# Another order of the first half of a hand-written instruction list, in attention and MLP on one core

## The chip, the core and the metric

The kernel runs on one core of one Trainium2 chip. The metric is device time in microseconds of one execution. A core has five engines with an instruction stream each: TensorE (PE in the profile, which also shows its weight loads as PEld), VectorE (DVE), ScalarE (ACT), GpSimd (POOL) and SyncE (SP, which here only issues DMAs). Each engine takes its instructions in order; engines wait for each other by semaphores.

## What is computed

Batch 8, 8 heads, 576 positions, head size 64; the model width is 512 and the MLP's 2048. The inputs are float32.

```python
scores = scale * np.matmul(q, k.transpose(0, 1, 3, 2))
cum = np.cumsum(np.maximum(s, 0.0), axis=-1)
bias = -(cum[:, :, :, None] - cum[:, :, None, :])
scores = np.where(causal, -1e9, scores + np.minimum(bias, 0.0))
attn = softmax(scores); x = np.matmul(attn, v)      # heads side by side: [8, 576, 512]
xn = (x - mu) / np.sqrt(var + 1e-06) * g_ln
out = x + np.maximum(xn @ w_ch1, 0.0) @ w_ch2
```

## The kernel before

All of it is in `fast_path` (lines 28 to about 1365). Work is cut into small steps, each a Python function that emits a few instructions. A dictionary `STEPS` (L1186) gives each step a short name, and a string `PLAN` (L1274, 1238 words) lists the steps in the order in which they are emitted. The order is written out: inside `tc.manual_schedule()` every engine executes its instructions in the order of emission, and nothing rearranges them. A word such as `E.k.4.1:D` is a step's name, its arguments, and after the colon the engine (A is ACT, D is DVE, P is POOL):

```python
for word in PLAN.split():
    step, _, eng = word.partition(":")
    name, *args = step.split(".")
    args = [int(c) if c.isdigit() else c for c in args]
    STEPS[name](*args, *([E[eng]] if eng else []))
```

The batches are treated in three ways.

- Batch 0, by tiles of 128 positions, while the data comes in. The sums of the gate (`relur`, `relu`, `scan` L292) are split into three bfloat16 pieces (`hi`, `mid`: L308, or L306 where ACT does it; `sub`, `lo`: L311), of which one scan has three parts (columns 0 to 128, to 256, to 576). `tc` transposes them on PE (L275), `bc` puts them beside q and k in `rowb` (DVE, L281 and L285), `ck` and `cq` cast the first tile of k and q (ACT, L140). `T` transposes a tile of q and k on PE (L944), `e` evicts it from PSUM (L140 on ACT, L142 on DVE), `S` makes scores (L966, mask L974), `x` the exponentials (ACT, L983), `V` the weighted sums (L1024), `N` divides them (DVE, L1049), `B` and `L` are the layernorm's statistics and its result xn (L710), `X` transposes xn on PE (L743), `y` evicts it, `M` is a piece of the first MLP layer (L1068), `r` its relu. `Sk`/`xk` are the scores and exponentials of the last 64 keys. `m` and `me` are memsets, the latter on POOL (L1235).
- Batch 1, by heads. `Q` transposes k or q of a head pair on PE (L322), `E` evicts it. `s` makes a head's scores in three PSUM banks (L390), their exponentials on ACT (L401) and a causal mask on POOL (L410); `d` the last 64 keys of a pair of heads (L426, L437, mask L440). `v` is the weighted sum (L583), `n` the division (DVE, L595, L597, L604). `aug` and `a3` copy bias rows by DMA. `O2`, `F` and `G` are cast, transposes (L360) and eviction for pairs of batch 2.
- Batches 2 to 7, by pairs of heads. The gate becomes a weight on v: `wr`, `wT`, `wx` make the weights, `vm` multiplies v by them on POOL (L232), `vo` writes the weights beside it (L244, L245). `lr` and `lv` load k, q, v in float32 (SP), `cr` casts k and q on POOL (L217), `tr` transposes them by DMA, `tk` copies the last keys on POOL (L144). `B2` is a burst of six banks of scores of a pair (L548), `bx` one bank's exponentials (ACT, L553), `bm` one mask (POOL, L492); `sd`, `se`, `sm` are the same for the last 64 keys. `Y` is the weighted sum (L627), `K` its division. `ga`, `la`, `l` are layernorm statistics and xn (L669, L710), `R` the reciprocal deviation of batch 0 (DVE L683, then POOL L684), `Da` and `D` its transposition by DMA on SP.

The MLP of the batches before is a queue of units. A word `u` or `U` takes the next unit: either "h", four matmuls of the first layer (L761) with their relu eviction, or "y", four matmuls of the second layer (L780); the last "y" of a tile adds the residual into `yo` (DVE, L792) and writes it out by a DMA on SP. The two words differ only in the engine of the relu eviction: ACT for `u` (L752), DVE for `U` (L750).

```python
"U": lambda: run_units(1, "dve"),
"u": lambda: run_units(1, "act"),
```

Most waits come from buffers. Until the word `to`, PSUM has two banks "m" (T, M, units), three "s" (scores), two "t" (Q, X, V, F, transposes) and one "o" (v); from `to` on there are two "m" (second layer) and six "s" (scores, first layer). A step that takes a bank waits until the step that used it before has been evicted. `lp` and `w2` issue DMAs on POOL's own stream (L183, L255), in which the masks stand too.

Of the kernel before, what the change touches and what calls it, by code (L numbers as in the profile page):

```python
# [30 lines left out]
def fast_path(  # L31
# [1147 lines left out]
    def raise_flag(count, ones, n):  # L1179
# [120 lines left out]
        la.1.4 B2.10 bx.10.0 K.9.0 bx.10.3 bx.10.4 bx.10.2 bx.10.5 cr.3.4.0 bm.10.3 bx.10.1 Y.9.1 U  # L1300
        K.9.1 u u tr.3.2.4 U u tr.3.4.5 bm.10.1 Y.10.1 lv.3.1 bm.10.0 B2.11 bx.11.0 bx.11.4 lv.3.2
        bx.11.5 lv.3.3 K.10.1 bm.10.2 Y.10.0 K.10.0 bm.11.2 ga.2.0.0 lv.3.4 bx.11.2 bm.11.0 La.4 bx.11.1
        u ga.2.1.2 ga.2.0.3 U u tk.3 cr.4.1.1 lr.4.2 bx.11.3 Y.11.0 K.11.0 bm.11.3 u sd.3 U bm.11.1 u
        se.3 ga.2.0.1 lr.4.3 cr.4.0.1 vm.3.1:P Y.11.1 K.11.1 lv.4.0 lv.4.1 vm.3.4:P lr.4.4 u ga.2.1.0 u
        B2.12 bx.12.0 vm.3.2:P U bx.12.4 bm.12.2 ga.2.1.1 bx.12.1 lv.4.2 ga.2.2.0 cr.4.2.1 ga.2.2.1
        ga.2.1.3 lv.4.3 la.2.0 la.2.1 cr.4.0.0 bx.12.5 bm.12.3 vm.3.3:P cr.4.1.0 ga.2.2.2 bx.12.3
        bm.12.1 u bx.12.2 bm.12.0 u u u B2.13 bx.13.5 bx.13.1 ga.2.0.2 la.2.2 u bx.13.0 cr.4.4.0 sm.3
        bx.13.4 tr.4.0.2 ga.2.2.3 u u bx.13.3 u Y.12.0 la.2.3 Da.2.0 bx.13.2 bm.13.0 K.12.0 u u B2.14
        cr.4.4.1 tr.4.4.5 bx.14.2 Y.12.1 K.12.1 lv.4.4 bx.14.1 bm.13.2 bx.14.3 vo.4:P bx.14.4 u u u
# [279 lines left out]
```

## Time and profile before

| | us |
|---|---|
| Three runs | 346.55, 347.80, 348.76 (median 347.80) |
| Profiled execution, own time | 347.71 |
| Its span, first to last instruction | 346.2 |
| PE waits by semaphore, the longest single one | 1.5 (before any data is there) |
| PE's waits after 8 us that the trace lists, together | about 4 |

Busy time of the engines over 40 equal slices of 8.65 us; a digit is tenths, 9 is 90% or more:

```profile
PE   5999999989999999999999999999999999999994
DVE  6598798847585587356653764567358614533512
ACT  4587889768655676357646773486434204202200
POOL 8898577696577774865685277350301001000000
```

The list's first 639 words fill the time to about 135 us, that is the first 15 to 16 slices. "Idle before" in a row of a timeline is the time in square brackets in which the engine did nothing, and behind the arrow stands what ended it; starts are counted from the first instruction.

### The profile page before, as it was taken

The page shows a single profiled execution, that of the slowest core. Times are in us where ns is not written, and L with a number is a line of the kernel's source. Part 1 is how long each engine was busy: PE and PEld are TensorE (multiplying, and loading weights), DVE is VectorE, ACT ScalarE, POOL GpSimd, SP SyncE. Part 2 cuts the span into 40 slices and gives each one's busy share as a digit, 9 for nine tenths or more (in the row PEclk, how much of TensorE's full clock was granted, in tenths as well). Part 3 has the DMA queues.
Part 4 walks back from the last instruction along what each step waited for, and adds up shares of the span by engine and source line. Part 5 has one row for each costly group of instructions (what it writes and reads, how often), then busy time and mean ns, then how long its engine had stood idle before and what let it go on. Part 6 is the DMA issues. An engine that isn't in the chain of part 4 may idle for free.

```text
span 346.2 us, 8012 instructions
## 1 busy us (share of the span) xinstructions
PE 332.7 (96%) x3066; PEld 186.3 (54%) x3092; DVE 206.2 (60%) x592; ACT 185.5 (54%) x343; POOL 167.8 (48%) x306
## 2 busy tenths in 40 slices
PE   5999999989999999999999999999999999999994
PEld 2898866545545555555555555555545444444443
DVE  6598798847585587356653764567358614533512
ACT  4587889768655676357646773486434204202200
POOL 8898577696577774865685277350301001000000
PEclk9699999999999999999999999999999999999999
DMA  9999999899999999998775956500410041011022
GB/s 148 181 192 176 203 206 204 171 247 218 199 203 232 221 222 180 224 230 187 154 197 145 236 104 159 138 2 2 118 66 0 20 134 45 2 66 56 0 64 66
DMA packets 147485, 48.61 MB, mean 140 GB/s; under 512 B 135184, under 2 KB 142896, under 8 KB 147440
## 3 DMA queue, kind: packets, MB, share of 16 engines
q1 hardware_dynamic: 121616, 38.34, 51.3%
q0 software_dynamic: 24304, 8.92, 21.8%
q10 hardware_dynamic: 1520, 0.79, 0.9%
q8 instruction: 25, 0.41, 0.5%
q14 instruction: 20, 0.16, 0.2%
HBM read 37.11 MB, written 9.44 MB: 134 GB/s over the span
## 4 chain that ended last, share of the span: by engine, by line
PE 89%; POOL 4%; DMA 4%; issue 1%; DVE 0%; ACT 0%; POOLq 0%
PE py L780 36%; PE ph L761 34%; PE pot L627 7%; DMA v_bf<-in_v_dram 2%; PE sa L548 2%; PE ph L1068 2%; DMA w_bf<-in_moe_w_ch_dram 2%; PE sc L548 2%; PE sb L548 2%; PE pot L583 1%; POOL rowb L179 1%; POOL kq L906 1%; PE trp L360 1%; PE trqk L322 1%; PE sb L390 1%
## 5 line engine op out<-in xcount | busy, mean ns | idle before, releaser
L780 PE MATMUL py<-w_bf,hT 128*128 128x512 bf16 (+2 forms) x583 | 128.3, 368 | 2.3 <-DVE yo L792 0.8
L761 PE MATMUL ph<-xT,w_bf 128*128 128x512 bf16 x480 | 109.8, 380 | 0.0
L752 ACT ACTIVATE hT<-ph 128x512 bf16<-128x512 f32 x97 | 58.1, 603 | 80.8 <-PE ph L761 79.4
L780 PEld LDWEIGHTS <-hT 128*128 128x128 bf16 x608 | 56.1, 98 | 61.7 <-issue 1.3
L761 PEld LDWEIGHTS <-w_bf 128*128 128x128 bf16 x544 | 50.9, 98 | 56.4
L492 POOL TENSOR_SCALAR_AFFINE_SELECT er<-er 128x256 bf16<-128x256 bf16 x96 | 38.6, 416 | 60.9 <-ACT er L553 45.9
L792 DVE SCALAR_TENSOR_TENSOR yo<-py,rstd,xb 128x512 f32<-128x512 f32 x32 | 24.0, 751 | 50.0 <-PE py L780 42.2
L750 DVE TENSOR_SCALAR hT<-ph 128x512 bf16<-128x512 f32 x39 | 26.8, 690 | 26.8 <-PE ph L761 25.9
L553 ACT ACTIVATE er<-sb 128x512 bf16<-128x512 f32 x48 | 28.2, 609 | 21.1 <-PE sb L548 15.2
L553 ACT ACTIVATE er<-sa 128x512 bf16<-128x512 f32 x48 | 28.6, 609 | 13.7 <-PE sa L548 10.9
L232 POOL TENSOR_TENSOR v_bf<-rowtmp,wt 128x512 bf16<-128x512 f32 (+1 forms) x30 | 32.4, 1086 | 2.3 <-DMA rowtmp<-in_v_dram 2.2
L553 ACT ACTIVATE er<-sc 128x512 bf16<-128x512 f32 x48 | 28.7, 613 | 4.1 <-PE sc L548 4.1
L627 PEld LDWEIGHTS <-er 128*128 128x128 bf16 x672 | 25.7, 97 | 9.5 <-issue 0.4
L627 PE MATMUL pot<-v_bf,er 128*128 128x66 bf16 x672 | 28.0, 194 | 0.1
L684 POOL TENSOR_TENSOR rstd<-rstd,mhalf 128x4 f32<-128x4 f32 (+1 forms) x8 | 8.8, 1098 | 38.2 <-DVE rstd L683 34.4
L644 DVE TENSOR_REDUCE sums<-pot 128x5 f32<-128x10 f32 x48 | 7.9, 166 | 30.5 <-PE pot L627 30.2
L710 DVE SCALAR_TENSOR_TENSOR xn<-xb,mv,gb 128x512 bf16<-128x512 f32 x28 | 24.3, 870 | 1.0
L217 POOL CAST kq<-rowtmp 128x512 bf16<-128x512 f32 (+1 forms) x30 | 19.8, 669 | 9.6 <-DMA rowtmp<-in_k_dram 8.5
L669 DVE BATCH_NORM_STATS2 stats<-xb 128x6 f32<-128x128 f32 (+1 forms) x84 | 23.7, 322 | 0.4
L647 DVE TENSOR_TENSOR xb<-pot,rinvs 128x256 f32<-128x256 f32 x48 | 20.4, 425 | 1.6
L548 PEld LDWEIGHTS <-kq 64*128 64x128 bf16 x360 | 11.3, 95 | 10.0 <-issue 4.7
L983 ACT ACTIVATE er<-st 128x512 bf16<-128x512 f32 x24 | 13.1, 604 | 4.4 <-PE st L974 3.0
(169 smaller groups left out, 397.0 us busy)
## 6 DMA issues: line engine op xcount, KB each, us to landing
out_dram<-yo SPq DMA_DIRECT2D x32, 256.0 KB
rowtmp<-in_v_dram SPq DMA_DIRECT2D x24, 256.0 KB
rowtmp<-in_k_dram SPq DMA_DIRECT2D x20, 256.0 KB
rowtmp<-in_q_dram SPq DMA_DIRECT2D x20, 256.0 KB
w_bf<-in_moe_w_ch_dram POOLq DMA_DIRECT2D x8, 512.0 KB, 9.0
kp<-in_k_dram POOLq DMA_DIRECT2D x8, 144.0 KB, 8.5
qp<-in_q_dram POOLq DMA_DIRECT2D x8, 144.0 KB, 8.9
v_bf<-in_v_dram POOLq DMA_DIRECT2D x8, 128.0 KB, 7.3
```

The costliest lines, as they stand in the source:

```text
L232: e.tensor_tensor(out=v_bf[b % 2][0:pn, t, :, 0:D], in0=loaded.pop(("v", b, t))[0:pn], in1=wt[0:pn, t, b, :].unsqueeze(2).to_broadcast([pn ...
L492: nc.gpsimd.affine_select(out=out, in_=out, compare_op=ALU.is_ge, fill=0.0, base=0, pattern=pattern, channel_multiplier=-1,)
L548: nc.tensor.matmul(a, lhsT=lhsT, rhs=rhs, start=True, stop=True)
L553: nc.scalar.activation(out=er[:, 2 * n % 4 + i, o : o + 512], in_=bank["B", n].pop((name, i)), func=ACT.Exp, scale=scale,)
L627: nc.tensor.matmul(pot[:, t, :], lhsT=cols, rhs=v_bf[b % 2][:, kb, h, :], start=(kb == 0), stop=(kb == t),)
L669: nc.vector.bn_stats(out=st[b][:, t, part, :], in_=x_tiles(b)[t][:, lo:hi])
L710: nc.vector.scalar_tensor_tensor(out=xn, in0=tiles[t], scalar=mvs[b][:, t, 0:1] if b > 0 else mean0[:, t : t + 1], in1=gb, op0=ALU.subtrac ...
L750: nc.vector.tensor_scalar_max(out=dst, in0=ph, scalar1=0.0)
L752: nc.scalar.activation(out=dst, in_=ph, func=ACT.Relu)
L761: nc.tensor.matmul(ph, lhsT=w1_bf[:, kd, fb * P : (fb + 1) * P], rhs=xT[:, :, kd, :], start=(kd == 0), stop=(kd == KD - 1),)
L780: nc.tensor.matmul(py[t], lhsT=hT[:, fb, t * P : (t + 1) * P], rhs=w2_bf[:, fb, c0:c1], start=(fb == 0), stop=(fb == FB - 1),)
L792: nc.vector.scalar_tensor_tensor(out=yo, in0=py[t], scalar=rs, in1=x[:, c0:c1], op0=ALU.mult, op1=ALU.add)
```

## The change

Only `PLAN` is edited. Of its 1238 words the last 599, from `qm` on, are the same. The 639 words before them are the same words in another order, except that seven `u` more have become `U`. Unit by unit the eviction moves from ACT to DVE in eleven places and from DVE to ACT in four (batches 0 to 2); no matmul, no load and no eviction is added or left out. Orders that are needed for buffers and data are kept. Cut to the parts that the prediction speaks of, with the rest of the lines left out:

```diff
-        relur.1 lr.3.0 relu.0 scan.0 scan.1 cq hi.0 qu.1 hi.1 sub.0 mid.0 lo.0 relur.2 sub.1 scan.2 W.2
-        tc.0 bc.0 ck.0 T.0.1 T.0.0 mid.1 lo.1 tc.1 e.0.1:D bc.1 T.1.1 hi.2 sub.2 e.0.0:A S.0.0.0 T.1.0
...
-        x.3.0.1 V.1.0 e.3.1:D qu.3 La.2 N.1.0 V.1.1 N.1.1 L.1 S.2.0.0 x.2.0.0 S.2.0.1 x.2.0.1 S.3.0.2
-        x.3.0.2 X.0 y.0:A S.3.1.2 S.2.1.1 x.2.1.1 V.2.0 N.2.0 x.3.1.2 X.1 y.1:D S.3.0.0 x.3.0.0 V.2.1
...
-        T.4.0 e.4.0:D X.2 y.2:D x.3.1.3 Q.k.4 E.k.4.0:D T.4.1 e.4.1:D x.3.1.0 S.4.0.1 x.4.0.1 S.4.0.0
-        M.0.2.0 M.0.2.2 x.4.0.0 M.0.2.3 V.3.1 E.k.4.1:D N.3.1 B.2.1 S.4.1.1 x.4.1.1 u d.8 L.3 M.0.2.1
-        Q.q.5 r.0.2:D B.1.0 s.8 u X.3 S.4.1.0 x.4.1.0 y.3:D Sk xk E.q.5.1:D E.q.5.0:A B.0.0 B.3.0 a3 u
-        v.8 qu.4 qu.5 Q.k.5 lp.9 E.k.5.0:D u E.k.5.1:D V.4.0 N.4.0 s.9 cr.3.0.1 n.8 V.4.1 N.4.1 Q.q.6
-        E.q.6.0:A u B.2.0 d.10 s.10 wr Q.k.6 E.k.6.0:D A.0 v.9 lp.10 w2.2 lr.3.1 E.k.6.1:D n.9 u U
...
-        F.k.8 v.14 ga.1.0.1 F.k.9 G.k.9:A n.14 U u A.3 R vm.2.0:P lr.3.2 v.15 cr.3.2.0 O2.k.11:A lv.2.1
...
-        F.k.11 G.k.11:A tk.2 qu.6 qu.7 F.q.10 G.q.10:A cr.3.3.1 vm.2.4:P to u lv.3.0 B2.8 bx.8.3 bx.8.0
-        vo.3:P bx.8.2 l.1 l.2 l.3 D u ga.1.0.4 u lr.4.0 lr.4.1 sd.2 se.2 sm.2 ga.1.1.4 bx.8.4 bm.8.2
+        relu.0 scan.0 lr.3.0 W.2 hi.0 sub.0 relur.1 ck.0 mid.0 lo.0 scan.1 hi.1 tc.0 sub.1 relur.2
+        scan.2 cq bc.0 mid.1 hi.2 sub.2 T.0.1 e.0.1:D mid.2 T.0.0 e.0.0:A lo.1 tc.1 lo.2 aug bc.1 T.1.1
...
+        S.1.0.0 qu.2 qu.3 T.2.1 e.2.1:D T.2.0 e.2.0:D V.0.0 V.0.1 N.0.1 x.1.1.1 m S.1.0.1 bc.4 x.1.0.0
+        S.2.1.2 x.2.1.2 x.1.0.1 N.0.0 S.2.1.1 x.2.1.1 T.3.0 e.3.0:D S.2.1.0 T.3.1 e.3.1:D V.1.0 x.2.1.0
+        W.1 V.1.1 S.2.0.0 x.2.0.0 S.2.0.2 x.2.0.2 N.1.1 S.3.0.2 x.3.0.2 S.2.0.1 x.2.0.1 B.0.1 L.0 N.1.0
+        L.1 S.3.1.2 S.3.0.1 x.3.0.1 La.6 B.1.1 X.0 y.0:A V.2.0 N.2.0 X.1 y.1:D x.3.1.2 S.3.0.0 M.0.0.0
...
+        B.3.0 X.2 qu.6 T.4.0 e.4.0:D y.2:D T.4.1 S.3.1.0 x.3.1.0 x.3.1.3 S.4.0.1 e.4.1:D M.0.2.0 M.0.2.3
+        M.0.2.1 Q.k.4 E.k.4.0:D M.0.2.2 S.4.1.1 x.4.1.1 V.3.1 N.3.1 E.k.4.1:D x.4.0.1 u S.4.0.0 x.4.0.0
+        B.2.1 Q.q.5 L.3 E.q.5.1:D r.0.2:D s.8 u d.8 E.q.5.0:A Sk xk u X.3 y.3:D S.4.1.0 x.4.1.0 v.8 n.8
+        Q.k.5 E.k.5.0:D V.4.0 N.4.0 lp.9 w2.2 w2.3 s.9 E.k.5.1:D u V.4.1 d.10 B.0.0 N.4.1 wr s.10 Q.q.6
...
+        La.3 La.2 n.11 cr.3.0.0 ga.1.0.1 A.0 lp.10 A.3 d.12 s.13 u d.14 wT s.14 A.1 v.12 n.12 U U
+        O2.k.9:A wx s.15 v.13 n.13 A.2 ga.1.0.3 U F.k.8 F.k.9 O2.q.9:A v.14 n.14 G.k.8:A ga.1.1.0 qu.7 R
+        ga.1.1.2 me vm.2.0:P O2.q.8:A lr.3.1 U u ga.1.1.3 cr.3.1.1 lv.2.1 vm.2.1:P G.k.9:A v.15 n.15
+        ga.1.2.1 F.q.9 ga.1.2.2 lr.3.2 O2.k.11:A u lv.2.2 lv.2.3 u F.q.8 cr.3.0.1 cr.3.2.1 G.q.9:A
+        cr.3.1.0 O2.q.11:A vo.2:P O2.k.10:A vm.2.3:P lv.2.4 vm.2.4:P lr.3.3 lr.3.4 G.q.8:A ga.1.0.0
+        ga.1.2.0 l.0 ga.1.2.3 vm.2.2:P cr.3.2.0 ga.1.0.2 ga.1.1.1 u u O2.q.10:A F.q.10 G.q.10:A F.k.10
+        l.1 u u u G.k.10:A F.q.11 F.k.11 G.q.11:A l.2 l.3 D tr.3.0.2 G.k.11:A tk.2 cr.3.3.1 cr.3.3.0 to
+        u lv.3.0 lv.3.1 B2.8 bx.8.0 bx.8.5 bx.8.3 bx.8.1 u bx.8.4 u u sd.2 bm.8.2 bm.8.3 bx.8.2 bm.8.0 u
+        u bm.8.1 lv.3.2 se.2 sm.2 cr.3.4.1 B2.9 bx.9.1 Y.8.1 bx.9.3 bm.9.1 bx.9.4 bm.9.2 bx.9.5 bx.9.2
...
```

More of the change, by code (lines that the diff above doesn't have):

```diff
@@ L1300, in fast_path @@
[L1300 to L1309, printed above, removed]
@@ new lines, in fast_path @@
+        bx.14.5 bx.14.1 bm.14.3 cr.4.3.1 bm.13.1 cr.4.3.0 bx.14.0 bm.14.0 bx.14.3 bm.14.1 cr.4.2.0
+        tr.4.2.4 B2.15 bx.15.0 bx.15.2 vm.4.4:P bm.15.0 bx.15.4 Y.13.1 bx.15.1 bx.15.3 bm.15.1 tk.4
+        bx.15.5 vm.4.1:P bm.15.2 U U u U U Y.14.1 K.14.1 u u bm.14.2 Y.14.0 K.14.0 K.13.1 ga.3.1.1
+        ga.3.1.0 bm.15.3 u sd.4 se.4 ga.3.0.2 u cr.5.0.0 vm.4.2:P Y.15.1 K.15.1 ga.3.0.1 vo.4:P lr.5.1
+        cr.5.1.0 B2.16 bx.16.0 bx.16.1 ga.3.1.3 bx.16.4 bm.16.2 La.4 Y.15.0 ga.3.1.2 K.15.0 bx.16.2
@@ new lines, in fast_path @@
+        lv.7.0 sm.6 ga.5.1.3 bx.24.4 bm.24.2 ga.5.2.0 u lv.7.1 La.5 ga.5.2.1 u u bx.24.2 bm.24.0
+        ga.5.1.1 U vm.6.4:P ga.5.1.0 la.5.0 bx.24.5 bx.24.1 bm.24.3 vm.7.0:P ga.5.0.4 lv.7.2 u bm.24.1
+        lv.7.3 ga.5.2.2 u u Y.24.0 Da.3.4 u u lr.7.4 cr.7.4.0 u ga.5.2.3 u cr.7.0.0 tr.7.0.2 cr.7.4.1
+        tr.7.4.5 lv.7.4 B2.25 bx.25.2 bx.25.4 vo.7:P bx.25.0 bx.25.5 bx.25.1 bx.25.3 bm.25.2 K.24.0
+        la.5.1 Y.24.1 u K.24.1 ga.5.0.2 u ga.5.1.2 la.5.2 u la.5.3 Da.5.0 cr.7.3.1 bm.25.1 u u u u
@@ L1356, in fast_path @@
+        u u u u u u u u u u u u u u u u
     """
```

110 lines of the change are left out of this document (51 added, 59 removed).

## The prediction, made before the changed kernel was run

> **What bounds the kernel now.** I read the totals first, then the waits of TensorE (PE), then the windows of its clock.
>
> ```profile
> span 346.2 us, 8012 instructions
> PE 332.7 (96%) x3066; PEld 186.3 (54%) x3092; DVE 206.2 (60%) x592; ACT 185.5 (54%) x343; POOL 167.8 (48%) x306
> PE 89%; POOL 4%; DMA 4%; issue 1%; DVE 0%; ACT 0%; POOLq 0%
> ```
>
> PE is busy for 96% of the span and holds 89% of the chain that ended last. The other four stay at 60% or less. The change leaves every matmul as it is, and the last 599 words of the list too. So it can change only what PE waits for up to about 135 us, and how long PE runs at half clock. From the trace's answer on the waits of PE, all of the span:
>
> ```profile
> PE trt L944 <- DVE rowb L285: 1.2, 1, 1.2
> PE py L780 <- DVE yo L792: 0.8, 1, 0.8
> PE trqk L322 <- DMA w_bf<-in_moe_w_ch_dram: 0.6, 1, 0.6
> PE trp L360 <- ACT kq L140: 0.5, 1, 0.5
> PE ph L1068 <- issue: 0.4, 1, 0.4
> ```
>
> (What waits, for what, us in total, times, longest.) All of these fall before 74 us, in the stretch that is reordered, and together they are 3.5 us: 1.0% of the time. A new order can hardly win more than that, apart from the clock; it can lose any amount by a new wait. The windows show the clock (busy us of the five engines, then PEclk, DMA share, GB/s):
>
> ```profile
> 4.74:8.15 3.41, 1.54 (x7) 0.48 (x5) 3.05 (x10) 2.01 (x5) 3.33 (x6) 1.00 1.66 171
> 8.15:11.57 3.42, 2.83 (x26) 2.65 (x27) 1.89 (x9) 1.65 (x3) 3.01 (x4) 0.50 2.08 184
> 11.57:14.98 3.41, 3.19 (x32) 2.87 (x32) 1.46 (x5) 1.79 (x3) 2.58 (x4) 0.50 2.38 172
> ```
>
> The clock is halved for two stretches of 3.41 us, after one in which PE was busy for 1.54 of 3.41.
>
> **The change part by part.**
>
> *The start (+0.25).* PE's first transposes, T.0.1, wait for the bias columns bc.0 on VectorE (DVE).
>
> ```profile
> 5.32 0.48 DVE L292 TENSOR_TENSOR_SCAN c_sc<-c_one,c_sc,hT 64x128 f32<-64x128 f32 x1
> 7.34 0.87 DVE L292 TENSOR_TENSOR_SCAN c_sc<-c_one,c_sc,c_in 64x320 f32<-64x320 f32 x1
> 8.14 0.16 DVE L281 COPY rowb<-trc 128x24 bf16<-128x24 bf16 x1
> 8.45 1.89 PE L944 MATMUL trt<-ident,rowb 128*68 128x128 bf16 x16 [1.25 <-DVE rowb L285]
> ```
>
> The new order puts scan.1 behind hi.0, sub.0, mid.0 and lo.0, but bc.0 still stands behind scan.2, DVE's longest piece here (0.87). The pieces ahead of bc.0 are the same; scan.1 now ends later, so hi.1 on ScalarE (ACT) and sub.1, which needs it, come later, and scan.2 with them. Followed row by row, bc.0 starts at 8.39 (an estimate). PE loses 0.25; bounds 0 and 0.5 (one more piece like scan.1, 0.48, ahead). tc.0 is done before that in both orders, and ck.0 and cq, moved on ACT, wait for their loads in both.
>
> PE then runs without a gap from 11.3 to 14.98, as now. [...]
>
> *15 to 26 us (+0.85).* The scores of batch 0 (S), their exponentials (x), sums (V, N) and the layernorm (L, X).
>
> ```profile
> 22.48 0.75 DVE L710 SCALAR_TENSOR_TENSOR xn<-xb,mean,gb 128x512 bf16<-128x512 f32 x1
> 23.29 0.40 PE L743 MATMUL trx<-ident,xn 128*128 128x128 bf16 x4 [0.27 <-DVE xn L710]
> 20.00:30.00 10.00, 9.01 (x189) 8.54 (x187) 8.39 (x28) 8.80 (x17) 9.87 (x19) 1.00 1.48 191
> ```
>
> DVE is 84% busy here, so its order tells. The memset m, bc.4, N.0.0, both e.3 and B.0.1 now stand ahead of L.0; L.1 follows L.0 and N.1.0 at once. I walked the new list word by word, each word starting when its engine is free and its inputs are done, with its duration of now: X.1 comes at about 24.5 beside 23.29 (an estimate; the times "by the walk" below are found in the same way). 0.25 of the 1.2 is the late start, 0.1 is filled by other PE work: +0.85. Bounds: 0, if the S words between fill it, and 1.6, two rows of 0.75.
>
> *26 to 58 us: waits that go (-1.85) and come (+0.75, +0.3).*
>
> ```profile
> 28.23 0.39 PE L743 MATMUL trx<-ident,xn 128*128 128x128 bf16 x4
> 29.23 0.42 PE L322 MATMUL trqk<-ident,kp 96*128 96x96 bf16 x6 [0.62 <-DMA w_bf<-in_moe_w_ch_dram]
> 35.94 0.22 PE L1068 MATMUL ph<-xT,w_bf 128*128 128x128 bf16 x1
> 36.54 1.01 PE L1068 MATMUL ph<-xT,w_bf 128*128 128x128 bf16 x15 [0.38 <-issue]
> 42.53 0.66 PE L390 MATMUL sb<-kq 68*128 68x64 bf16 x2
> 43.03 0.38 PE L390 MATMUL sc<-kq 68*128 68x320 bf16 x2
> ```
>
> Q.k.4 starts at 29.23; the four transposes before it need 0.22 of PE, so 0.78 is lost. The DMA named was long done: Q.k.4 lacks a PSUM buffer until y.2 has emptied one. In the new list T.4.0, T.4.1, S words and M.0.2.0 stand between. M's wait at 36.54 (0.54 after 35.94 plus one matmul) is for y.3, which now has the S.4.1.0 and v.8 words behind it. sc follows sb 0.50 later at two matmuls (0.22), so 0.28 goes, since a unit now parts the scores; I count 0.25 for a later head with the same pattern, an estimate. Sum -1.85; bounds -1.85 and -0.6 (Q.k.4's alone, in part). New: T.4.1 and M.0.2 behind r.0.0 and y.2, s.8 behind E.k.4.1, d.10 behind E.k.5.1, a unit's bank. Each is part of one copy (0.3 to 0.69 us), worked out as 0.1 to 0.3 each: +0.75, bounds 0 and 1.6.
>
> lp.10, two DMA issues, is moved ahead of d.12's mask on POOL; w2.2 and w2.3 ahead of those of s.9 and s.10.
>
> ```profile
> 45.23 0.64 POOL L183 DMA_DIRECT2D kp<-in_k_dram  x1
> 46.49 0.79 POOL L255 DMA_DIRECT2D w_bf<-in_moe_w_ch_dram  x1
> 51.52 0.90 POOL L410 TENSOR_SCALAR_AFFINE_SELECT er<-er 128x256 bf16<-128x256 bf16 x2 [0.74 <-ACT er L401]
> ```
>
> 2 x 0.64 = 1.28 ahead of that mask leaves it done at about 54.35 by the walk, where PE wants v.12 at 54.05: +0.3, bounds 0 and 0.9 (a mask's length). The two w2 (2 x 0.79) end at 43.6 by the walk, s.10's masks at 45.5, and PE wants v.10 at 46.9: hidden by 1.4. What SP issues (aug, a3, lr, lv) runs ahead of the list and waits only for buffers: a3, now later, has been free to go since batch 0's last scores at 35, and s.12, its user, comes after 50: hidden.
>
> *58 to 76 us (-0.85).* The casts O2, transposes F and copies G of the next batch.
>
> ```profile
> 68.40 0.38 PE L360 MATMUL trp<-ident,rowb 96*128 96x96 bf16 x5
> 69.25 0.42 PE L360 MATMUL trp<-ident,rowb 96*128 96x96 bf16 x6 [0.47 <-ACT kq L140]
> 69.72 0.81 PE L780 MATMUL py<-w_bf,hT 128*128 128x512 bf16 x3
> 73.10 1.02 PE L780 MATMUL py<-w_bf,hT 128*128 128x512 bf16 x4 [0.84 <-DVE yo L792]
> ```
>
> F.q.10 now waits for a G copy (0.63 lost between 68.40 and 69.25 beyond the five matmuls, 0.21 after it). The new list does F.q.10 earlier and parts F.k.10 from F.q.11 by four units: -0.85; bounds -0.85 and -0.2. The wait for yo at 73.10 stays: the same units come before and after `to`.
>
> *POOL behind R (+0.55).* R (pow), the weightings vm, the casts cr, me, vo.2, tk.2 and the masks bm.8, sm.2 form one queue.
>
> ```profile
> 63.72 0.61 POOL L217 CAST kq<-rowtmp 128x512 bf16<-128x512 f32 x1 [0.94 <-DMA rowtmp<-in_k_dram]
> 65.90 1.04 POOL L232 TENSOR_TENSOR v_bf<-rowtmp,wt 128x512 bf16<-128x512 f32 x1 [1.57 <-DMA rowtmp<-in_v_dram]
> 69.17 2.49 POOL L232 TENSOR_TENSOR v_bf<-rowtmp,wt 128x512 bf16<-128x512 f32 x2 [0.66 <-DMA rowtmp<-in_v_dram]
> 60.71:77.81 17.10, 15.68 (x137) 8.03 (x138) 10.92 (x24) 11.57 (x21) 13.64 (x23) 1.00 0.91 210
> L1235 POOL MEMSET c<- 128x640 bf16 x2 | 1.2, 631 | 0.0
> 78.11 0.58 PE L627 MATMUL pot<-v_bf,er 128*128 128x66 bf16 x14
> ```
>
> From R to the last of these masks POOL is busy 13.64 of 17.10; about 3.2 of the rest are three waits for DMAs. The list now also puts me (1.2) and two more casts (2 x 0.61) into this stretch: 16.0 of work. R starts at about 61.1 by the walk (behind n.14 on DVE), so the masks end at 77.1 without waits and at 80.6 with all 3.46. PE wants them for Y.8 (L627) at 77.2 by the walk, 78.11 now. The loads lr.3 and lv.2 wait for buffers that these same casts empty; vo.2, me and two casts of tiles loaded long before now stand between, which gives them time. So most waits should go: I take about a sixth, which makes +0.55. Bounds 0 and 4.4 (all waits, and another 1.0 as the pair at 69.17 shows: 2.49 where 2 x 1.04 would do).
>
> ```profile
> 69.24 1.53 DVE L710 SCALAR_TENSOR_TENSOR xn<-xb,mv,gb 128x512 bf16<-128x512 f32 x1
> ```
>
> Beside that pair L710 took 1.53 (0.75 at 22.48). [...]
>
> *Seven evictions (0).*
>
> ```profile
> L752 ACT ACTIVATE hT<-ph 128x512 bf16<-128x512 f32 x97 | 58.1, 603 | 80.8 <-PE ph L761 79.4
> L750 DVE TENSOR_SCALAR hT<-ph 128x512 bf16<-128x512 f32 x39 | 26.8, 690 | 26.8 <-PE ph L761 25.9
> ```
>
> ACT sheds 7 x 0.60 = 4.2, DVE gains 7 x 0.69 = 4.8. What hides it is that a unit takes PE longer (four matmuls at 0.22) than the copy takes, with two to six banks in turn. Uncovered, seven copies longer by 0.09 cost 0.6; where ACT is late, as much is won: bounds -0.6 and +0.6. The rest, 76 to 135 us: tr.3.4.5 moves ahead of lr.4.0 on SP, which delays batch 4's loads to about 84 by the walk, wanted at 91; Da.2.0 comes at about 107, wanted at 115. Nothing: bounds 0, since none of the waits listed lies there, and +0.84, one wait like that at 73.10.
>
> Sum: 0.25 + 0.85 - 1.85 + 0.75 + 0.3 - 0.85 + 0.55 = 0.0. The profiled execution took 347.71, 0.09 under the median of 347.8: I forecast 347.7.
>
> **The rivals.**
>
> 1. Slower: POOL's queue behind R makes Y.8 wait. It decides from masks later than 77.3. For it: 16.0 of work where 13.64 stood, and L710 beside it. Against: most of its waits were for late loads. Price 4.4 in place of 0.55: 351.6; with half, 349.3.
> 2. Faster: the old waits go (-2.7) and the new ones are covered, since many words of other PE work stand between. With start and POOL as summed: 347.7 - 0.85 - 0.75 - 0.3 = 345.8; with X.1 and POOL free too, 345.0. The clock a stretch of 3.41 earlier adds -1.7, half of it: 343.3.
> 3. The clock a stretch longer, if PE idles about 11.3: +1.7, 349.4.
> 4. The change does nothing that can be told: the forecast's own number, by another way.
>
> **How the numbers follow.** My forecast (with rival 4) has 0.50, its own range 346.2 to 349.2 from the bounds of the small terms. Rival 1 has 0.25, rival 2 0.17, rival 3 0.08. About 1% (344.2, 351.2) is what a measurement of this kernel can tell from no change. Below 344.2 lies about half of rival 2: 0.09. Above 351.2 lie the full price of rival 1, and new waits in the long list that I did not find: 0.20. The rest, 0.71, is within 1%. The range leaves out the earlier clock and the full queue with more: 344.8 to 351.6.
>
> **What would show it.** Right: T.0.1 starts at 8.6 to 8.8; X.1 near 24.5; no gaps at Q.k.4, M after Sk and F.q.10; the gap at yo stays near 0.8; masks bm.8 and sm.2 end before Y.8 starts; PEclk back at 14.98. Wrong: a gap of over 1 us ahead of Y.8 or v.12, a third halved stretch or only one, or a gap after 80 us, where I charge nothing. A gap with other work of PE in the list right behind it, which could have filled it, would also tell against the walk.

## The result and the profile after

| | before | after |
|---|---|---|
| Median of 6 runs, us | 347.88 | 351.44 |
| Lowest and highest | 346.55, 348.76 | 350.27, 352.25 |
| Profiled execution, own time and span | 347.71, 346.2 | 351.36, 349.7 |
| Its mean granted clock | 0.990 | 0.983 |

The ratio is 1.0101, with a 95% interval of 1.0070 to 1.0131: the new order is 3.6 us slower. I had forecast 347.7 and no change. (The section on the change says eleven and four for the moved evictions; it is twelve and five, net seven.)

The changed kernel's totals, and then its list of PE's waits:

```profile
span 349.7 us, 7999 instructions
PE 336.2 (96%) x3067; PEld 188.8 (54%) x3092; DVE 209.6 (60%) x599; ACT 181.2 (52%) x336; POOL 167.7 (48%) x306
```

```profile
PE trt L944 <- DVE rowb L285: 2.1, 1, 2.1
PE py L780 <- DVE yo L792: 0.8, 1, 0.8
PE trx L743 <- ACT kq L140: 0.7, 1, 0.7
PE trx L743 <- DVE xn L710: 0.5, 1, 0.5
PE trt L944 <- DVE rowb L281: 0.3, 1, 0.3
PE sa L390 <- issue: 0.2, 1, 0.2
```

Two things are to be seen. PE's busy time grew by 3.5 us, from 332.7 to 336.2, though it has the same matmuls: by 0.6 ahead of T.0.1, in idle matmuls, and by 2.6 between T.0.1 and X.1, where it worked longer at half clock. And the list of waits has other names but about the same length: those for the weights' "DMA" (L322), for the G copy (L360) and the gap ahead of M behind Sk (L1068) are gone, and the first transposes (2.1 in place of 1.2) and X (0.7 and 0.5) took their place. The windows of the clock in the changed kernel:

```profile
6.50:9.92 3.42, 1.25 (x16) 1.03 (x17) 2.62 (x8) 2.42 (x7) 3.34 (x6) 0.99 1.71 185
9.92:13.33 3.41, 2.90 (x28) 2.53 (x26) 2.08 (x6) 1.46 (x2) 2.34 (x4) 0.50 2.40 154
13.33:16.74 3.41, 3.41 (x35) 3.15 (x34) 0.34 (x2) 1.99 (x3) 3.06 (x5) 0.50 1.99 196
16.74:20.16 3.42, 3.42 (x39) 3.42 (x38) 1.31 (x3) 1.57 (x3) 3.42 (x5) 0.51 1.56 198
20.16:23.57 3.41, 3.35 (x62) 3.00 (x61) 3.15 (x14) 2.08 (x5) 3.27 (x10) 1.00 1.69 176
```

The clock (third number from the end) is halved for three stretches in place of two, and PE is fully busy in the last two, so here half clock is time lost.

To place the loss, I took for some words the start of their first matmul less all of PE's work that stands ahead of it in the same list, at full rate by the rows (0.056 for 128 columns, the distance of the starts from 9.38 to 9.77 in the changed kernel; 0.216 for 512, that from 5.03 to 5.25 in the kernel before). What is left is the time that PE has lost up to there, by waiting or by half clock. Idle matmuls (W) in the list count as work. It can be compared between kernels even where words stand in another order. It is good to about 0.1 us.

| lost time at | before | after | start_back | to26_back |
|---|---|---|---|---|
| T.0.1 | 7.89 | 8.54 | 8.07 | 7.99 |
| X.1 | 12.29 | 15.93 | 12.94 | 11.16 |
| X.2 | 12.41 | 16.86 | 13.87 | 11.46 |
| d.10 | 13.80 | 17.80 | 14.82 | 12.61 |
| v.12 | 14.20 | 17.97 | 14.98 | 12.78 |
| B2.8 | 14.94 | 18.19 | 15.20 | 12.99 |
| first Y.8 | 15.97 | 19.28 | 16.39 | 14.23 |

After against before: +3.64 up to X.1, +0.36 from there to d.10, -0.23 to v.12, -0.46 to Y.8, and +0.05 to the kernel's own check near the end (L1181, 330.37 beside 327.01). So all of it is lost in the first 27 us, and a third of a microsecond comes back later.

### The profile page after: what moved, and what is told of

Read it like the earlier page. It is cut to its first block, busy times and chain, and to the rows that moved or that the text cites. A ratio compares the mean times of both kernels' runs of the same rounds, so it can differ in the third digit from the quotient of the medians.

```text
span 349.7 us, 7999 instructions
## 1 busy us (share of the span) xinstructions
PE 336.2 (96%) x3067; PEld 188.8 (54%) x3092; DVE 209.6 (60%) x599; ACT 181.2 (52%) x336; POOL 167.7 (48%) x306
## 4 chain that ended last, share of the span: by engine, by line
PE 77%; issue 0%; DVE 0%
PE py L780 33%; PE ph L761 32%; PE pot L627 7%; PE sa L548 2%; PE sc L548 2%; PE sb L548 2%; PE sd L519 0%; DVE yo L792 0%; PE count L1181 0%
## 5 line engine op out<-in xcount | busy, mean ns | idle before, releaser
L780 PE MATMUL py<-w_bf,hT 128*128 128x512 bf16 (+2 forms) x583 | 128.1, 367 | 2.2 <-DVE yo L792 0.8
L752 ACT ACTIVATE hT<-ph 128x512 bf16<-128x512 f32 x91 | 54.3, 604 | 80.6 <-PE ph L761 79.1
L780 PEld LDWEIGHTS <-hT 128*128 128x128 bf16 x608 | 56.0, 98 | 61.9 <-issue 1.3
L750 DVE TENSOR_SCALAR hT<-ph 128x512 bf16<-128x512 f32 x45 | 30.8, 689 | 27.1 <-PE ph L761 26.3
L232 POOL TENSOR_TENSOR v_bf<-rowtmp,wt 128x512 bf16<-128x512 f32 (+1 forms) x30 | 33.3, 1115 | 0.2
```

The source lines that it names most:

```text
L232: e.tensor_tensor(out=v_bf[b % 2][0:pn, t, :, 0:D], in0=loaded.pop(("v", b, t))[0:pn], in1=wt[0:pn, t, b, :].unsqueeze(2).to_broadcast([pn ...
L750: nc.vector.tensor_scalar_max(out=dst, in0=ph, scalar1=0.0)
L752: nc.scalar.activation(out=dst, in_=ph, func=ACT.Relu)
L780: nc.tensor.matmul(py[t], lhsT=hT[:, fb, t * P : (t + 1) * P], rhs=w2_bf[:, fb, c0:c1], start=(fb == 0), stop=(fb == FB - 1),)
```

## The experiments

Each kernel was timed beside the kernel before on the same chip; the ratio is to that. Different kernels ran on different chips, where the kernel before took 347.77 to 348.13; so where two medians differ by little, the ratios count. Two theories. One: the start, and with it the half clock, costs most of it. The rival: the order of batch 0's words behind the start (15 to 33 us), through VectorE, does.

**start_back.** The first 33 words in the old order among themselves, the rest as in the changed kernel:

```diff
-relu.0 scan.0 lr.3.0 W.2 hi.0 sub.0 relur.1 ck.0 mid.0 lo.0 scan.1 hi.1 tc.0 sub.1 relur.2 scan.2 cq bc.0 ...
+relur.1 lr.3.0 relu.0 scan.0 scan.1 cq hi.0 hi.1 sub.0 mid.0 lo.0 relur.2 sub.1 scan.2 W.2 tc.0 bc.0 ck.0 ...
```

> The changed kernel with its first 33 words (to T.1.0) put back into the old order among themselves. Clock theory (PE's late first transposes, 9.10 beside 8.45, make the half clock last three stretches of 3.41 in place of two): T.0.1 back at 8.4 to 8.5, half clock for two stretches, time 351.4 - 0.6 - 1.8 = 349.0. Rival, that the number of stretches is chance from run to run and not the order's: only the 0.6 comes back, 350.8, and the granted clock stays near 0.983. Rival, that the order of 15 to 33 us costs it all: 351.4.

349.28 (1.0039, 1.0020 to 1.0059): 2.16 less than the changed kernel, as the clock theory said. T.0.1 came at 8.63 and T.1.1 at 10.12 (11.28 in the changed kernel). In the profiled execution the clock was halved for one stretch:

```profile
10.12:13.54 3.42, 3.42 (x33) 3.42 (x33) 1.49 (x4) 1.58 (x4) 2.69 (x5) 0.50 2.43 154
13.54:17.00 3.46, 3.46 (x63) 3.24 (x62) 1.39 (x4) 2.95 (x5) 3.17 (x4) 1.00 1.89 199
```

The mean granted clock over its ten runs is 0.9925; over the six of the changed kernel it is 0.9832. Single executions at the same mean clock (0.986 and 0.987) lie closer together: 350.27 and 350.42 in the changed kernel, 349.68 and 350.02 here. So, as far as four executions can tell, most of the 2.16 goes with the clock and about 0.5 does not.

**to26_back.** The first 116 words in the old order among themselves; only the order behind them is new.

> The changed kernel with its first 116 words (to Q.q.4) in the old order among themselves; the new order from there. If all of the loss lies ahead of 27 us, and the new order wins 0.3 to 0.7 behind it (the trace shows PE's lost time growing by 0.6 less there): 347.9 - 0.5 = 347.4, clock 0.990. If the waits behind 27 us come back in another place: 348.5 or more.

347.44 (0.9990, 0.9973 to 1.0008), as expected: the two stages together hold the loss. The start costs 2.16 (351.44 to 349.28), the order from there to Q.q.4 1.84 (349.28 to 347.44), and behind it the new order wins 0.33, which is within the interval.

**after_warm and before_warm.** Idle matmuls where PE waits for bc.0:

```diff
-scan.1 hi.1 tc.0 sub.1 relur.2
+scan.1 hi.1 tc.0 W.8 sub.1 relur.2
```

> The changed kernel with eight more idle matmuls (W.8) behind tc.0, where PE idles for 2.07 us ahead of T.0.1; their result is not used. Clock theory: PE is busy in the stretch before 9.92, so the clock isn't halved, and up to 5.1 us of half speed goes: PE then waits for its inputs instead, so 347 to 349. If the halving doesn't come from that idle time: 351.4 or a little more.

> The kernel before with five more idle matmuls (W.5) behind tc.0, where PE idles for 1.25 us ahead of T.0.1. Clock theory: busy share of the stretch 4.74 to 8.15 rises from 1.54 to 2.6 of 3.41; if that holds the clock, up to 3.0 us of half speed goes, less the waits that follow: 345 to 347, clock near 1.00. If not: 347.9.

after_warm: 348.61 (1.0014, 0.9997 to 1.0030), 2.8 less than the changed kernel, at a mean clock of 0.997. before_warm: 347.81 (1.0008, 0.9986 to 1.0030), no change, at 0.998. So the half clock was taken away in both, and it was worth 2.8 in the one and nothing in the other. In the kernel before, PE at full clock ran into its inputs: before_warm's list of waits has 0.3 at L322 for a copy on ACT, 0.3 at L780 for "DMA" and 0.2 at L322 for DVE, which the kernel before's has not. The five added idle matmuls (1.08) count as work in the lost time; with them taken as lost too, it is 10.16 at X.1 (12.29 without them), 11.83 at v.12 (14.20) and 14.27 at the first Y.8 (15.97). Of 2.1 won up to X.1, 1.45 are left at the check near the end (325.56 beside 327.01). That is in the profiled execution, the shortest of the ten (346.84); in the medians nothing is left.

**ck0_later.** One word moved:

```diff
-... relur.1 ck.0 mid.0 lo.0 scan.1 hi.1 tc.0 ...
+... relur.1 mid.0 lo.0 scan.1 hi.1 ck.0 tc.0 ...
```

> The changed kernel with one word moved: ck.0 (ACT's cast, which waits for k until 6.71) behind hi.1, so that hi.1, sub.1, scan.2 and bc.0 no longer wait for that load. By the row before sub.1 this frees 0.36. Theory that the late T.0.1 is the cause and the third half-clock stretch hangs on it: T.0.1 at 8.7, time 351.4 - 0.4 to 351.4 - 2.1, that is 349.3 to 351.0. Rival, that the warm matmuls ahead of relur and scan set the phase: 351.0 and the clock as it was, 0.983.

351.47 (1.0095, 1.0069 to 1.0122): nothing. T.0.1 came no earlier (9.38 in the profiled execution): hi.1 started when scan.1 was done (7.05), so sub.1 still waited 0.36 for it, and scan.2 now waited 0.61 for relur.2, which stands behind ck.0 on ACT. So this run says nothing on what an earlier T.0.1 would be worth.

**start_parts.** VectorE's order at the start put back in part, ACT's ck.0 left where it is:

```diff
-relu.0 scan.0 lr.3.0 ... relur.1 ck.0 mid.0 lo.0 scan.1 hi.1 ... mid.1 hi.2 sub.2 ... lo.1 tc.1 lo.2 aug bc.1
+relur.1 relu.0 scan.0 scan.1 lr.3.0 ... ck.0 mid.0 lo.0 hi.1 ... mid.1 lo.1 hi.2 sub.2 ... tc.1 bc.1 lo.2 aug
```

> The changed kernel with relur.1 and scan.1 back in the old place (scan.1 right behind scan.0), lo.1 right behind mid.1 and lo.2 behind bc.1; ck.0 stays ahead of hi.1. Theory that DVE's order alone, ahead of bc.0 and bc.1, makes the start late: T.0.1 at 8.7, T.1.1 at 10.4, time as start_back, 349.3, clock 0.992. Rival, that it is ACT's order (ck.0 and cq): T.1.1 after 11.0 and 351.

349.49 (1.0033, 1.0011 to 1.0054), clock 0.9915; T.0.1 at 8.79, T.1.1 at 10.32. ACT's own order is as in the changed kernel. So it is DVE's order: scan.1 behind four short pieces, and lo.1 and bc.1 behind sub.2, e.0.1 and lo.2.

**before_newstart and before_late.** The converse of start_back, and a late T.0.1 alone (m ahead of scan.2 in the kernel before):

```diff
-... lo.0 relur.2 sub.1 scan.2 W.2 tc.0 bc.0 ... T.1.0 W.1 m mid.2 ...
+... lo.0 relur.2 sub.1 m scan.2 W.2 tc.0 bc.0 ... T.1.0 W.1 mid.2 ...
```

> The kernel before with its first words (the new list's first 33 without aug) in the new order among themselves, all else as before: the converse of start_back. Theory that the start's order costs 2.2 by itself (its late T.0.1 and T.1.1, and longer half clock): 347.8 + 2.2 = 350.0, mean granted clock 0.984 to 0.986. Rival, that the cost needs the new order of the S words behind it: 347.8 + 0.6 = 348.4, clock 0.991.

> The kernel before with one word moved: the memset m (0.51 + 0.07 on DVE) ahead of scan.2, so that bc.0 and T.0.1 come 0.6 later, at 9.0 as in the changed kernel; all other order as before. Theory that PE's longer idle time at the start lengthens the half clock: 347.8 + 0.6 + 1.7 = 350.1, clock 0.987 or less. Rival, that a late T.0.1 costs only itself: 348.4; or that waits behind it take it up: 347.8.

before_newstart: 348.60 (1.0022, 1.0002 to 1.0043) at a mean clock of 0.9852. The clock fell as the first theory said, and the time rose by 0.8 and not by 2.2: the loss was taken up behind it, where the old order has waits to fill (0.78 at Q.k.4 is gone, lost time 14.51 at X.2 and at Q.k.4). So the price of the start depended on what stood behind it: 0.8 with the old order, 2.2 with the new one. before_late: T.0.1 at 9.51 and 348.08 (1.0012, 0.9992 to 1.0032), clock 0.990: a late T.0.1 alone cost nothing that can be told and didn't move the clock (0.991 in the kernel before, over the 29 executions beside it). That part of the theory fell.

**mB_later and dve_early.** What makes X.1 late. In mB_later m and B.0.1 stand behind L.1. In dve_early the words that feed DVE stand ahead of scores:

```diff
-tc.2 bc.2 qu.1 S.1.1.1 x.0.1.0 S.1.1.0 x.1.1.0 S.1.0.0 ... T.2.1 e.2.1:D T.2.0 e.2.0:D V.0.0 V.0.1 N.0.1 x.1.1.1 m S.1.0.1 bc.4 x.1.0.0
+tc.2 bc.2 m bc.4 qu.1 S.1.1.1 x.0.1.0 V.0.0 N.0.0 T.2.1 e.2.1:D S.1.1.0 x.1.1.0 T.2.0 e.2.0:D V.0.1 N.0.1 S.1.0.0 ... x.1.1.1 S.1.0.1 x.1.0.0
```

> The changed kernel with the memset m (0.51 + 0.07 on DVE) and the statistics B.0.1 (0.42) moved behind L.1. Theory that DVE's order ahead of L.0 and L.1 makes X.1 late: X.1 comes 0.9 earlier, its wait of 0.52 goes, time 351.4 - 0.5 to - 0.9 = 350.5 to 350.9. Rival, that the exponentials on ACT bind 20 to 27 us: X.1 the same or within 0.2, 351.4.

> The changed kernel with the first words that feed VectorE moved ahead: V.0.0, N.0.0, T.2.1, T.2.0, V.0.1 and N.0.1 stand among the S.1 words and not behind them, m and bc.4 directly behind bc.2, B.0.1 behind L.1. In the changed trace DVE idles 5.3 us between 13 and 18.7 and is then full to 28. Theory that this is why X.1 is late: PE's lost time between V.0 and X.1 falls from 2.4 to about 0.9 (the kernel before's), 351.4 - 1.5 = 349.9. Rival, that the scores' banks and the exponentials on ACT hold X.1 instead: 350.9, what moving m and B.0.1 alone gave.

mB_later: 351.14 (1.0094, 1.0059 to 1.0128), not to be told from the changed kernel; in its trace the lost time from V.0.0 to X.1 is 1.79, where start_back and yo_fill, with the same words in between and the clock also back by then, have 2.39. X.1's wait for xn is gone, but one of 0.6 for its buffer, copied on ACT, has come. dve_early: 349.89 (1.0071, 1.0042 to 1.0100), less than the changed kernel by 1.5 in the medians and by 1.0 in the ratios, and its interval overlaps the changed kernel's; so the time can't part the theory (349.9) from the rival (350.9). Its trace speaks against the theory: from V.0.1 to X.1 it loses 1.90 (12.61 to 14.51), as the changed kernel does from S.2.1.2 on (14.02 to 15.93), and the wait at X.1 now has another name. (What the trace does gain is at X.2: 0.43 from X.1 to T.4.1 in place of 0.93.)

```profile
25.51 0.38 PE L743 MATMUL trx<-ident,xn 128*128 128x128 bf16 x4 [0.57 <-ACT xT L140]
```

The two windows that had led to it, of the kernel before and then of the changed one:

```profile
12.40:18.70 6.30, 6.08 (x92) 5.76 (x92) 3.62 (x14) 4.15 (x7) 5.85 (x8) 0.80 1.81 191
18.70:28.20 9.50, 9.13 (x187) 8.76 (x185) 8.41 (x27) 8.72 (x17) 9.37 (x18) 1.00 1.53 191
```

```profile
12.40:18.70 6.30, 6.30 (x62) 6.04 (x61) 1.03 (x4) 3.50 (x6) 5.75 (x8) 0.50 1.84 193
18.70:28.20 9.50, 8.72 (x141) 7.76 (x140) 8.76 (x30) 6.32 (x13) 9.36 (x18) 0.93 1.52 191
```

DVE (third engine of the row) works 1.03 of the first 6.30 us in the changed kernel, where it worked 3.62, and is then nearly full; but ACT (fourth) is behind as well, with 0.65 less in the first and 2.4 less in the second window. Both are fed late. In that first window PE itself ran at clock 0.50, where it had 0.80 in the kernel before.

**dve_new and dve_old.** To part the two, behind start_back's start and up to Q.q.4: in dve_new PE's and ACT's words stand in the old order and DVE's in the new one among themselves, in dve_old the other way round. A cut of each against to26_back and start_back:

```diff
-T.2.0 S.1.0.1 x.1.0.1 e.2.0:D V.0.1 S.1.0.0 N.0.1 S.2.1.2 x.2.1.2 T.3.0 x.1.0.0 e.3.0:D
+T.2.0 e.2.0:D S.1.0.1 x.1.0.1 V.0.1 N.0.1 m bc.4 N.0.0 S.1.0.0 S.2.1.2 x.2.1.2 T.3.0 e.3.0:D x.1.0.0
```

```diff
-T.2.1 e.2.1:D T.2.0 e.2.0:D V.0.0 V.0.1 N.0.1 x.1.1.1 m S.1.0.1 bc.4 x.1.0.0
+T.2.1 T.2.0 V.0.0 N.0.0 bc.4 e.2.1:D e.2.0:D V.0.1 N.0.1 x.1.1.1 S.1.0.1 x.1.0.0
```

> start_back, and behind it, up to Q.q.4, the old order of PE's and ACT's words with the new order of VectorE's words among themselves (bc, m, N, B, L, copies on DVE). start_back has 349.3, to26_back 347.4. Theory that VectorE's own order makes X.1 late: 349.0 to 349.3, lost time at X.1 near start_back's 12.9. Rival, that the order of scores and exponentials (PE, ACT) does: 347.4 to 347.8, lost time at X.1 near 11.2 to 11.7.

> start_back, and behind it, up to Q.q.4, the new order of PE's and ACT's words with the old order of VectorE's words among themselves. Theory that VectorE's own order makes X.1 late: 347.4 to 347.8, lost time at X.1 near 11.2 to 11.7. Rival, that the order of scores and exponentials does: 349.0 to 349.3, lost time at X.1 near 12.9. If both cost a half: 348.4 in both kernels.

dve_new: 349.54 (1.0031, 1.0005 to 1.0057). dve_old: 350.07 (1.0051, 1.0033 to 1.0069). Neither theory holds: each half of the new order loses by itself about as much as the whole of it (start_back, 349.28), and the 1.84 come back only with both halves old. Part of this is the clock. The lost time at X.1 is 14.27 and 14.58, above both forecasts, and both profiled executions ran longer at half clock than start_back's (up to 14.25 and 14.93, where it had 13.56). But at about the same mean clock the loss is still there: dve_new's four executions at 0.990 and 0.991 took 348.60 to 348.95, to26_back's three there 347.59 to 347.74; dve_old's five at 0.994 and 0.995 took 349.15 to 349.90, to26_back's four at 0.993 and 0.994 346.56 to 347.57. The waits show how, of dve_new and then of dve_old:

```profile
20.54 0.40 PE L966 MATMUL st<-kq 68*128 68x128 bf16 x4 [0.69 <-DVE kq L142]
23.46 0.40 PE L743 MATMUL trx<-ident,xn 128*128 128x128 bf16 x4 [1.14 <-DVE xn L710]
```

```profile
19.03 0.23 PE L966 MATMUL st<-kq 68*128 68x128 bf16 x1 [1.03 <-DVE kq L142]
25.59 0.38 PE L743 MATMUL trx<-ident,xn 128*128 128x128 bf16 x4 [0.58 <-ACT xT L140]
```

With DVE's new order PE waits for a copy of q and k and for X.0's xn. With PE's and ACT's new order it waits for another such copy, which DVE's old order has late, and for X.1's buffer on ACT. Each order fits the others of its own list.

**X2_later.** X.2's new wait of 0.70, filled with 1.1 us of transposes and scores:

```diff
-X.2 qu.6 T.4.0 e.4.0:D y.2:D T.4.1 S.3.1.0 x.3.1.0
+qu.6 T.4.0 e.4.0:D T.4.1 S.3.1.0 X.2 y.2:D x.3.1.0
```

> The changed kernel with X.2 and y.2 moved behind S.3.1.0, so that T.4.0, T.4.1 and S.3.1.0 (1.1 us of PE) stand where X.2 waits 0.70 for the second copy of E.q.4 on ACT. Theory that this new wait is paid in full: 351.4 - 0.7 = 350.7. Rival, that the next wait for the same PSUM buffers (Q.k.4 behind y.2, as in the kernel before) takes its place: 351.4.

351.19 (1.0079, 1.0052 to 1.0106). The interval holds both forecasts, so the trace has to tell. The lost time from X.1 to d.10 is 1.88 (16.09 to 17.97), where the changed kernel has 1.87: other waits took its place in full, as the rival said, but not the one at Q.k.4 that it named. T.4.1 now waits, and so does M.0.2 behind y.2:

```profile
32.30 0.50 PE L944 MATMUL trt<-ident,rowb 96*68 96x96 bf16 x8 [0.44 <-DVE hT L1081]
33.82 0.83 PE L1068 MATMUL ph<-xT,w_bf 128*128 128x128 bf16 x12 [0.28 <-DVE xT L142]
```

**evict_back.** The seven evictions, undone by units (17 words swapped between u and U).

> The changed kernel with every MLP unit evicted on the engine that it has in the kernel before (17 unit words swapped), the order unchanged. The prediction's step, that these evictions cost nothing: 351.4, PE's waits as in the changed kernel. Rival, that VectorE's slower copies hold PE's banks: 350.8 or less.

351.98 (1.0121, 1.0089 to 1.0153): no gain, and none of PE's waits went. The evictions cost nothing that can be told.

**yo_fill and yo_pool.** The wait for yo that both kernels have, filled with the burst, and then POOL's queue behind it relieved:

```diff
-to u lv.3.0 lv.3.1 B2.8 bx.8.0 bx.8.5 bx.8.3 bx.8.1 u bx.8.4
+to u lv.3.0 lv.3.1 u B2.8 bx.8.0 bx.8.5 bx.8.3 bx.8.1 bx.8.4
```

> The changed kernel with one unit word moved ahead of B2.8, so that the burst stands between the end of output tile 2 and the start of tile 3 of batch 0, where PE waits 0.8 to 1.0 for yo in both kernels. Theory that this wait is paid in full: 350.5. Rival, that the burst's exponentials and masks then come 0.9 later and Y.8 waits for them: 351.4 or more.

> The changed kernel with the burst B2.8 behind the end of output tile 2, as in yo_fill, and with three casts of batch 3 (cr.3.1.0, cr.3.2.0, cr.3.2.1) and tr.3.0.2 moved behind sm.2 on POOL. In yo_fill the wait for yo fell from 0.84 to 0.35 and sd.2 waited 0.71 for tk.2 in POOL's queue, which runs without a pause from 62 to 80. Theory that this queue is what stands behind the yo wait: both go, PE's lost time from v.12 to Y.8 falls from 1.3 to about 0.4, time 351.4 - 0.9 = 350.5. Rival, that loads or G copies hold tk.2: no change to yo_fill's trace.

yo_fill: 350.44 (1.0069, 1.0045 to 1.0094); yo_pool, with three casts and tr.3.0.2 behind sm.2 as well: 349.89 (1.0067, 1.0037 to 1.0097). The first trace has no gain in this stage (lost time 1.33 from v.12 to Y.8, 1.31 in the changed kernel): the wait at yo shrank, and another one came,

```profile
73.53 1.89 PE L780 MATMUL py<-w_bf,hT 128*128 128x512 bf16 x8 [0.35 <-DVE yo L792]
76.13 0.41 PE L519 MATMUL sd<-kq,kz 128*128 128x64 bf16 x8 [0.71 <-POOL kz L144]
```

for tk.2 in POOL's queue, which is busy for 17.21 of the 17.50 us from R on:

```profile
62.40:79.90 17.50, 16.32 (x161) 8.74 (x161) 11.29 (x26) 11.33 (x20) 17.21 (x28) 1.00 0.89 196
```

With the casts out of the way both waits are gone in yo_pool (lost time 0.2 in the stage), and the next is the transposition of batch 1's xn by DMA:

```profile
79.23 2.12 PE L761 MATMUL ph<-xT,w_bf 128*128 128x512 bf16 x9 [0.49 <-DMA xT<-xn]
```

Little of this gain reaches the end: the ratios of the two kernels are the same, and at the check near the end (L1181) yo_pool's PE is 0.23 ahead (328.14 beside 328.37). That yo_fill's median is lower than the changed kernel's at all is not explained by its edit: its profiled execution had one half-clock stretch and not three.

**best1.** to26_back with the edits of yo_pool.

> to26_back (old order to Q.q.4, new order behind it) with the edits of yo_pool. Both gains together: 347.4 - 0.9 = 346.5, about 0.4% under the kernel before. If the run's clock or a load decides instead: 347.4.

347.60 (1.0000, 0.9985 to 1.0016). The gains do not add: in its trace PE waits 0.72 for the same DMA, and 0.67 ahead of a V (L1024) at 39.71. No kernel that was tried is faster than the kernel before by more than the measurement can tell; to26_back comes nearest.

## Why the prediction was wrong, step by step

**The start (+0.25), the step that failed.** With the new order behind it, it cost 2.16 (351.44 to 349.28 in start_back). As far as T.0.1 the walk was short by 0.4:

```profile
4.76 0.28 DVE L1192 SCALAR_TENSOR_TENSOR hT<-hT 64x128 f32<-64x128 f32 x1 [0.93 <-DMA hT<-in_s_dram]
7.62 0.28 DVE L311 TENSOR_TENSOR hT<-c_sc,c 64x128 f32<-64x128 f32 x1 [0.36 <-ACT c L306]
9.10 1.24 PE L944 MATMUL trt<-ident,rowb 128*68 128x128 bf16 x16 [2.07 <-DVE rowb L285]
10.73 0.26 PE L275 MATMUL trc<-ident,c 96*128 96x96 bf16 x1 [0.23 <-DVE c L311]
11.28 1.92 PE L944 MATMUL trt<-ident,rowb 128*68 128x128 bf16 x16 [0.29 <-DVE rowb L281]
```

0.28 of it is s, which landed later in this execution (relu.0 at 4.76, 4.48 before). Without that, bc.0 came 0.37 later than in the kernel before (8.79 beside 8.14), where the walk had 0.25: sub.1 waited 0.36 for hi.1. But before_late shows that this is not where the 2.16 comes from: there T.0.1 came at 9.51, and it cost nothing that can be told.

What failed is that the clock had no term in the sum; only rivals 2 and 3 had one. I expected "PEclk back at 14.98", with PE "without a gap from 11.3 to 14.98, as now". PE did run without a gap from 11.28, and the clock came back at about 20.1. The longer half clock was rival 3, at 0.08, with the price of one stretch, 1.7 (an estimate, half of 3.41; that idle time about 11.3 alone would bring the stretch, no run shows). That the new start brings it, whatever stands behind, is shown by the means over all executions: 0.983 to 0.989 in the nine kernels with the new start (0.983 in the changed kernel, 0.985 in before_newstart, at the upper end 0.987 in yo_pool and 0.989 in yo_fill), 0.990 to 0.9925 in those with the old one and in start_parts (kernels with added idle matmuls left out). And after_warm shows that it costs: without the half clock the changed kernel takes 2.8 less. What in DVE's order does it is narrowed to scan.1, lo.1 and bc.1 (start_parts), not to one word, and how it does it stays open.

**15 to 26 us (+0.85): right sign, half the size, and only half the mechanism.** It measured 1.84 (start_back to to26_back). I walked DVE's words, found them late for L.1, and PE does wait there for xn (0.52). But DVE's order is not the cause by itself: with the old one put back (dve_old) the loss stays, and PE waits for the copy of q and k and for ACT. The walk took PE's and ACT's new order as filled time; dve_old shows that it has waits of its own. Which pairs of words must stand as they did is open.

**Waits that go (-1.85) and come (+0.75, +0.3): failed.** The waits at Q.k.4, after Sk (but for 0.2) and within d.10's scores did go, but the sum from X.1 to v.12 is +0.13 in place of -0.8. The new waits are as large as the old: 0.87 lost at X.2, whose PSUM buffer waits behind two copies on ACT (the row above it in time),

```profile
30.41 1.59 ACT L140 COPY kq<-trqk 64x576 bf16<-64x576 bf16 x2
```

```profile
32.05 0.38 PE L743 MATMUL trx<-ident,xn 128*128 128x128 bf16 x4 [0.70 <-ACT kq L140]
```

and 0.4 at s.8. I had found X.2's neighbours and not X.2, and X2_later shows that finding it would not have helped: with X.2's wait filled, 1.88 is lost from X.1 to d.10, as before. That the chain of copies through the two "t" banks binds the stage is my reading; no run shows it. lp.10 ahead of d.12's mask cost nothing at v.12. (The bound of 0.9 called "a mask's length" is the row's two instructions together.)

**58 to 76 us (-0.85) and POOL (+0.55): about right together.** -0.46 in place of -0.3. F.q.10's wait went; the wait for yo stayed at 0.84. The masks of POOL's queue ended just in time:

```profile
76.67 0.60 POOL L217 CAST kq<-rowtmp 128x512 bf16<-128x512 f32 x1
77.22 0.85 POOL L144 COPY kz<-kq 64x256 bf16<-64x256 bf16 x2
80.71 0.65 POOL L492 TENSOR_SCALAR_AFFINE_SELECT c<-c 64x512 bf16<-64x512 bf16 x1
```

sm.2 ends at 81.36, and PE's matmul that reads it starts at 81.42. Beside l.0 and l.3 the vm words took 0.44 and 0.36 longer (1.48 from 68.14, three in 3.48 from 73.23, at 1.04 each before), 0.8 of the 1.0 that the bound had. R came at 64.40, 3.3 later than in the walk, and PE was later too (first Y.8 at 80.95, 77.2 by the walk). yo_fill shows that rival 1's queue was there, covered by the wait at yo: PE waits for it at sd.2 and for 0.71, not at Y.8 for 4.4. (Rival 2's two totals hold a slip: 345.8 leaves out X.1's 0.85 already, and 345.0 leaves out the 0.25 of the start and the 0.55 of POOL. Nothing else hangs on it.)

**Evictions and the rest (0): right.** evict_back shows no gain, and from Y.8 to the end the lost time grows by the same amount in both kernels to 0.05.

The start's order did not fix the number of stretches at half clock. With the new one, single profiled executions had one (yo_fill, mean clock 0.994), two (mB_later, 0.987), three (the changed kernel, 0.983) and four (evict_back, 0.976, from 7.55 to 21.20). Over runs the order did shift the mean (0.9832 in the changed kernel, 0.9925 in start_back), and this was worth some 2 us with the new order behind it.

## What to carry to other kernels

A reorder at the start of a kernel needs a term for the clock in its sum. Here another order of VectorE's first words cost about 2 us (351.44 beside 349.49 in start_parts), most of it by a longer half clock (mean clock 0.9832 beside 0.9915). A late first transpose alone did not lengthen it (before_late, 0.990), and idle matmuls in the gap took it away (after_warm, 0.997, and before_warm, 0.998). What taking it away was worth depended on the waits behind: 2.8 us in one kernel, nothing in the other. A stage that three engines share was fitted as a whole: one engine's order in it can't be judged alone (dve_new, dve_old). And here, with PE 96% busy, a wait that went was mostly replaced by the next one behind it (X2_later: 1.88 lost from X.1 to d.10, 1.87 in the changed kernel; yo_fill: 1.33 from v.12 to Y.8, 1.31 in the changed kernel; mB_later: 0.6 for X.1's buffer in place of 0.5 for xn), so credit a removed wait only after naming the next bound and its time.
